# A GEGLU block with adaptive layer norm on Trainium2: a written plan for three engines in the gate and up passes, the differences on VectorE, and gb applied at the end of the down stage

## The chip, the core and the metric

The kernel runs on one core of one Trainium2 chip. The time is that of one execution on the device, in microseconds (us); the number given for a kernel is the median of its runs. The core has five engines that run their own instruction queues: TensorE (PE, with its weight loads as PEld), VectorE (DVE), ScalarE (ACT), GpSimd (POOL) and SyncE (SP), whose queue issues all the kernel's DMAs. An instruction that needs another engine's result waits for a semaphore at the head of its queue.

## The reference

T = 2048 tokens, D = 1024 columns, F = 3584 hidden columns, all in float32. It is cut here to what the change touches.

```python
mod = (silu(c) @ w_mod).reshape(1, 6, 1, -1)
sa, ca, ga, sb, cb, gb = (mod[:, i] for i in range(6))
h = layernorm(x) * (1 + ca) + sa
x = x + ga * attention(h)              # 32 heads, 4 segments with a running memory
h = layernorm(x) * (1 + cb) + sb
x = x + gb * ((gelu(h @ w_gate) * (h @ w_up)) @ w_down)
```

## The kernel before

**Stages.** Attention and its output projection come first, up to 1191.5 us in the profiled execution. The projection's last blocks (`projections`, `project`, L614 to L705) write x1, the sum after attention, to HBM; beside them the second norm writes h2, normalised and transposed, to HBM, and the first operands of the feed-forward part are cut. Then follow gate and up (L954, to 2363 us) and down (L1019, to the end).

**Numbers in two parts.** Each operand of a matmul is held as a high part (ScalarE copies float32 to the matmul's shorter type, L749) and a low part (the difference to the original, L751), and a product is three matmuls: high x high, high x low, low x high.

**Seven products instead of eight.** Gate and up of one block of 128 hidden columns are computed together as a 2 x 2 by 2 x 2 block product in a form with seven multiplications. The operands A are made from the blocks of h2 (two halves of D by two halves of 512 tokens); the operands B from the blocks of w_gate and w_up for these 128 columns (b11, b21 of gate, b12, b22 of up). Sums and differences of blocks stand in for the eighth product: for B four differences (`t1`, `t2_` and two more, L904 to L918), and as many for A. The products are numbered and run in the order `PRODUCTS = (1, 6, 2, 7, 5, 4, 3)`. The down stage does the same with sums of the hidden blocks and of w_down's blocks.

**Rounds.** There are two passes over the F columns, one for each half of the tokens (NP = 2, TP = 1024), with 28 blocks of 128 columns each (FC = 28): 56 rounds, numbered m = 0 to 55, in `gate_up(m)`. In a round each product is 12 matmuls of 128x128 by 128x512 (four pieces of 128 rows by three high and low pairings). Three PSUM banks `pa`, `pb`, `pc` take the products, and several products are added onto one bank: product 1 to `pa`, then ScalarE copies it to c1 (L979), then product 2 is added onto it. After product 6, 7, 5, 4 and 3 VectorE reads a bank (L981, L987, L989, L991, L994); TensorE may not add the next product onto a bank before it has been read. Such a reading is called a taking below. VectorE then multiplies the two GELU values by the two sums (L995, L996), and the result `g` is stored to HBM.

**Work beside the products.** Four kinds share the engines with the takings:

- `b_part(m + 2)`: the tables of a later round are loaded (`rg`, `ru`, 512 KB each), the four differences are made by GpSimd (`diff`, L762), the seven high parts by ScalarE, and the low parts by VectorE except two (products 5 and 3), which are GpSimd's.
- `w_parts`: in the first pass, for 14 pairs of w_down's blocks: VectorE multiplies them by gb (L938), GpSimd makes four differences (L762), and the results go to HBM as `wT_d`.
- the second norm for the second half of the tokens (`norm_tiles`, with TensorE's transposes `tpb`), the sums of its blocks (`a_mix`), and at the end of the first pass the 28 operands A for the second pass (`a_next`).
- `sum_part`: in the second pass, sums of a round's result with earlier ones (`sc`, L1014): two instructions in each of the first 14 rounds, six in each of the last 14.

**Order.** TensorE and SP run in the order in which the program is written. For SP the steps of `sides` (generators advanced by `step()` after every half product) and of `late` place the DMA issues. For VectorE, ScalarE and GpSimd a planner decides: it orders instructions by its own estimate of when they can start. Two further places matter. The operands A of the first pass are cut in `a_first`, `a_second` (before the stage, its rows in the two buffers `ra`, one pair at a time) and `a_last` (at its start). And the row gb, spread over all partitions by two pairs of matmuls with a matrix of ones (`row_parts`, L161), is computed at the start of the stage, between the first matmuls of round 0. In the down stage (`down`) the last additions read x1 and a PSUM bank and store the output: `final`, called first with no bank (GpSimd adds a stored sum to x1, L1083) and then with one (L1085).

Of the kernel before, what the change touches and what calls it, by code (L numbers as in the profile page):

```python
# [19 lines left out]
P = 128  # L20
D = 1024
# [15 lines left out]
def block_kernel(ctx: ExitStack, tc: tile.TileContext, x, c, wmod, wq, wkv, wo, beta, wg, wu, wd, out):  # L37
# [636 lines left out]
    def projections():  # L674
# [17 lines left out]
        sides.append([ff["b"](0), 2, "b"])  # L692
# [11 lines left out]
        next(ff["b1"])  # L704
# [14 lines left out]
    def feed_forward():  # L719
# [21 lines left out]
        A, B, hid, done = {}, {}, {}, set()  # L741
# [6 lines left out]
        def cut(hi, lo, src, eng, behind=False):  # L748
            i = [nc.scalar.activation(hi, src, AF.Copy)]  # L749
            for k in parts(src.shape[-1], eng):  # L750
                i.append(eng.tensor_sub(lo[:, k], src[:, k], f32(hi)[:, k]))  # L751
            if behind:
                keep(*i[:2])

# [5 lines left out]
        def diff(dst, a, b):  # L760
            for k in parts(dst.shape[-1], nc.gpsimd):
                nc.gpsimd.tensor_sub(dst[:, k], a[:, k], b[:, k])  # L762

        def put_a(p, i, kt, src, eng, behind=False):
            hl = [a_tile(i, kt, q, f"A{p}_{i}_{kt}_{q}") for q in range(2)]
            cut(hl[0], hl[1], src, eng, behind)
            A[p, i, kt] = hl
# [13 lines left out]
        def a_mix(p):  # L781

            for kt in range(4):
                r = rows(p, kt, ra_tile, "rm")
                for _ in range(4):
                    yield
                a11, a21, a12, a22 = r[0][:, :L], r[0][:, L:], r[1][:, :L], r[1][:, L:]
                s1 = tmp_tile(f"m1_{p}_{kt}")
                s2 = tmp_tile(f"m2_{p}_{kt}")
                for i, t, f in ((5, s1, lambda: nc.vector.tensor_add(s1, a21, a22)),  # L790
                                (6, s2, lambda: nc.vector.tensor_sub(s2, s1, a11)),
                                (7, a21, lambda: nc.vector.tensor_sub(a21, a11, a21)),
                                (3, a12, lambda: nc.vector.tensor_sub(a12, a12, s2))):
                    f()
                    later(3, lambda i=i, t=t, kt=kt: nc.sync.dma_start(mix_rows(i)[kt * P:(kt + 1) * P], t))
                    for _ in range(4):
                        yield

        def a_next(p):

            tok = p * TP
            todo = [(i, b) for i in PRODUCTS for b in range(2)]
            rs = []

            def load():
                q = len(rs)
                if q < len(todo):
                    i, b = todo[q]
                    src = (mix_rows(i) if i in MIX else
                           h2_d[0 if i == 1 else L:L if i == 1 else D, tok + (L if i == 4 else 0):tok + (TP if i == 4 else L)])  # L810
                    get = ra_tile if q % 3 == 2 else raw_tile
                    t = get(f"ra{p}_{i}_{b}").rearrange("p (k t) -> p k t", k=2)
                    nc.sync.dma_start(t, src[2 * b * P:(2 * b + 2) * P].rearrange("(k p) t -> p k t", p=P))
                    rs.append(t)

            for _ in range(5):
                load()
            yield
            for q, (i, b) in enumerate(todo):
                while (p * FC - 1, i) not in done:  # L820
                    yield
                for k in range(2):
                    put_a(p, i, 2 * b + k, rs[q][:, k], nc.vector)
                    if k:
                        load()
                    yield

        def a_first():
# [4 lines left out]
            for kt in range(4):  # L833
                r = rs[kt]
                a11, a21, a12, a22 = r[0][:, :L], r[0][:, L:], r[1][:, :L], r[1][:, L:]
                put_a(0, 1, kt, a11, nc.vector, True)
# [5 lines left out]
                put_a(0, 6, kt, s, nc.vector, True)  # L842
                yield
                put_a(0, 2, kt, a12, nc.vector, True)
# [6 lines left out]
        def a_second():  # L851

            rs = [rows(0, kt, ra_tile, "rb") for kt in range(1)]
            for _ in range(3):
                yield
            for kt in range(4):
                r = rs[kt]
                a11, a21, a22 = r[0][:, :L], r[0][:, L:], r[1][:, L:]
                s = tmp_tile(f"s5_{kt}")
                keep(nc.vector.tensor_add(s, a21, a22))  # L860
                nc.gpsimd.tensor_sub(a21, a11, a21)
                if kt < 2:
                    put_a(0, 4, kt, a22, nc.gpsimd)
                yield
                put_a(0, 7, kt, a21, nc.vector, True)
                yield
                put_a(0, 5, kt, s, nc.vector, True)
                if kt < 3:
                    rs.append(rows(0, kt + 1, ra_tile, "rb"))
                yield  # L870
                yield

        def a_last():

            r = ra_tile("rc").rearrange("p (k t) -> p k t", k=2)
            nc.sync.dma_start(r, h2_d[D - 2 * P:D, L:TP].rearrange("(k p) t -> p k t", p=P))
            for kt in range(4):
                (h2, l2), (h6, l6) = ([f32(t) for t in A[0, i, kt]] for i in (2, 6))
                s1 = tmp_tile(f"s1_{kt}")
                s2 = tmp_tile(f"s2_{kt}")  # L880
# [451 lines left out]
```

## Time and profile before

| what | value |
|---|---|
| median of 3 runs | 2915.62 us (2914.53 to 2917.37) |
| the profiled execution | 2912.03 us, its span 2910.3 us |
| granted TensorE clock in it | 0.985 of full speed |
| busy in the span: PE, DVE, ACT, POOL | 2771.3, 1671.9, 1310.4, 1179.4 us |
| gate and up | first matmul 1191.5 us, last one starts at 2362.6 us |
| DMA | 480.39 MB, 165 GB/s in the mean |

The profile is of one execution. In a table of windows each row gives a stretch of the span, its length, then the busy time of each engine with its number of instructions, the granted clock of TensorE, the mean busy share of the DMA queues' engines, and GB/s. A row of groups reads: line, engine, operation, output <- inputs, shape, count, then busy time and the mean time of one in ns, then the idle time of the engine just before them and what ended it. A row of waits reads: who waited <- for what: us in total, times, longest. A row of the timeline reads: start, length, engine, line, operation, and in brackets the idle time before it.

### The profile page before, as it was taken

To read this page: it belongs to the slowest core of one execution; us is meant where nothing else is said; L and a number is where in the kernel's file an instruction comes from. 1 tells how busy PE (TensorE), PEld (TensorE's weight loads), DVE (VectorE), ACT (ScalarE), POOL (GpSimd) and SP (SyncE) were. 2 spreads that over 40 slices of the span, in tenths; PEclk is the share of its full clock that TensorE was granted. 3 is DMA by queue.
4 is the path that set the end of the run, shared out by engine and by line. 5 is a ranking of instruction groups with operands and counts; after the bars stand their busy time and mean duration, and the time that the engine had idled before them with its cause. 6 is when DMAs were issued, how large, how long until landed. Compare 5 with 4: busy or idle time off the path is not lost.

```text
span 2910.3 us, 41951 instructions
## 1 busy us (share of the span) xinstructions
PE 2771.3 (95%) x14716; PEld 2286.9 (79%) x14716; DVE 1671.9 (57%) x3366; ACT 1310.4 (45%) x2871; POOL 1179.4 (41%) x1696
## 2 busy tenths in 40 slices
PE   5999999999999999799989998999999989999999
PEld 4788888888888787577767887888877778888887
DVE  7565666766666824555556555655677763334442
ACT  6677766676666634244422334333323233232221
POOL 0333334333343422466668763644566611102221
PEclk8999999999999999899999999999999999999999
DMA  7567666766555657455566434344456575544652
GB/s 239 113 131 145 144 109 131 145 137 115 108 112 98 168 174 232 147 196 202 188 210 222 164 113 167 144 145 145 171 227 239 223 244 185 195 145 147 202 187 92
DMA packets 229875, 480.39 MB, mean 165 GB/s; under 512 B 17696, under 2 KB 92448, under 8 KB 229664
## 3 DMA queue, kind: packets, MB, share of 16 engines
q1 hardware_dynamic: 229664, 477.72, 55.7%
q8 instruction: 115, 1.88, 0.3%
q14 instruction: 96, 0.79, 0.1%
HBM read 300.96 MB, written 126.35 MB: 147 GB/s over the span
## 4 chain that ended last, share of the span: by engine, by line
PE 69%; DVE 9%; POOL 7%; DMA 6%; ACT 4%; issue 4%; SPq 0%; DVEq 0%; POOLq 0%; ACTq 0%
PE f L962 25%; PE d L1142 18%; PE kv L365 10%; PE q L371 3%; PE y L626 3%; PE T L556 3%; POOL wt L762 3%; PE S L492 2%; PE O L565 2%; POOL t L762 2%; POOL B L751 1%; ACT sj L496 1%; DVE qs L509 1%; DMA wd<-wd 1%; DVE sj L494 1%
## 5 line engine op out<-in xcount | busy, mean ns | idle before, releaser
L962 PE MATMUL f<-A,B 128*128 128x512 f32 x4704 | 1098.0, 394 | 57.6 <-DVE c L981 34.6
L962 PEld LDWEIGHTS f<-A,B 128*128 128x128 f32 x4704 | 889.7, 190 | 258.8 <-DVE c L981 43.8
L1142 PE MATMUL d<-wb,ah 128*128 128x512 f32 x2352 | 536.6, 391 | 7.0 <-DVE wb L1052 3.7
L1142 PEld LDWEIGHTS d<-wb,ah 128*128 128x128 f32 x2352 | 443.5, 189 | 100.1 <-DVE wb L1052 4.2
L494 DVE CUSTOM_DVE_ANT_0 sj<-S,mask 128x384 f32<-128x384 f32 (+3 forms) x512 | 229.6, 487 | 226.1 <-PE S L492 207.6
L496 ACT ACTIVATE sj<-sj,mm 128x384 f32<-128x384 f32 (+3 forms) x512 | 281.4, 551 | 113.5 <-DVE mm L494 113.2
L559 POOL TENSOR_SCALAR_AFFINE_SELECT pt<-pt 128x128 f32<-128x128 f32 x512 | 170.7, 354 | 338.2 <-ACT pt L558 332.6
L749 ACT ACTIVATE B<-t 128x512 fp32r<-128x512 f32 x168 | 106.0, 631 | 291.8 <-PE f L962 219.7
L1052 DVE TENSOR_TENSOR ah<-ar,ah 128x1792 fp32r<-128x1792 f32 x56 | 118.5, 2116 | 196.6 <-ACT ah L1051 189.7
L1051 ACT ACTIVATE ah<-ar 128x1792 fp32r<-128x1792 f32 x56 | 95.3, 1702 | 278.5 <-PE d L1142 255.8
L365 PE MATMUL kv<-w,hha 128*128 128x256 f32 x1024 | 205.1, 286 | 3.4 <-ACT hha L334 3.4
L365 PE MATMUL kv<-w,hhh 128*128 128x256 f32 x1024 | 202.7, 286 | 0.0
L201 POOL TENSOR_TENSOR w<-r,w 128x256 fp32r<-128x256 f32 x180 | 133.3, 771 | 166.3 <-ACT w L196 166.2
L558 ACT ACTIVATE pt<-T 128x256 f32<-128x256 f32 (+3 forms) x512 | 181.9, 456 | 38.1 <-PE T L556 33.9
L365 PEld LDWEIGHTS kv<-w,hha 128*128 128x128 f32 x1024 | 167.7, 192 | 4.7 <-ACT hha L334 4.3
L365 PEld LDWEIGHTS kv<-w,hhh 128*128 128x128 f32 x1024 | 167.4, 193 | 0.3 <-issue 0.2
L751 POOL TENSOR_TENSOR B<-t,B 128x256 fp32r<-128x256 f32 x112 | 87.3, 800 | 167.3 <-ACT B L749 161.7
L365 PE MATMUL kv<-w,hla 128*128 128x256 f32 x512 | 146.4, 286 | 5.9 <-DVE hla L335 4.2
L556 PE MATMUL T<-qs,ks 128*128 128x256 f32 (+2 forms) x512 | 128.1, 360 | 20.1 <-DVE qs L509 7.6
L556 PEld LDWEIGHTS T<-qs,ks 128*128 128x128 f32 x512 | 80.8, 190 | 84.2 <-issue 35.1
L762 POOL TENSOR_TENSOR t<-rg,t 128x256 f32<-128x256 f32 x112 | 100.6, 918 | 111.1 <-DVE B L751 111.1
L365 PE MATMUL kv<-w,hlh 128*128 128x256 f32 x512 | 145.6, 284 | 0.0
(217 smaller groups left out, 4563.7 us busy)
## 6 DMA issues: line engine op xcount, KB each, us to landing
ar<-hid_d SPq DMA_DIRECT2D x56, 896.0 KB, 5.1
rg<-wg SPq DMA_DIRECT2D x56, 512.0 KB, 5.8
ru<-wu SPq DMA_DIRECT2D x56, 512.0 KB, 6.4
hid_d<-g SPq DMA_DIRECT2D x56, 512.0 KB, 2.7
sc<-hid_d SPq DMA_DIRECT2D x56, 512.0 KB, 5.0
hid_d<-sc SPq DMA_DIRECT2D x56, 512.0 KB, 3.1
br<-wT_d SPq DMA_DIRECT2D x49, 512.0 KB, 6.0
ks<-kh SPq DMA_DIRECT2D x64, 256.0 KB, 5.6
```

What stands on the lines that cost most here:

```text
L201: eng.tensor_sub(w[:, 1, k:k + 256], r[:, k:k + 256], f32(w[:, 0, k:k + 256]))
L365: nc.tensor.matmul(ps, b[:, sl], w[:, a], start=(kt == 0 and a == 0 and b is hi), stop=(kt == KT - 1 and a == 1), **kw)
L494: nc.vector.tensor_tensor_reduce(out=sj[:, :nv], in0=ps[:, :nv], in1=mask[:, L - nv:], scale=-1.0, scalar=3.4e38, op0=ALU.add, op1=ALU.min ...
L496: nc.scalar.activation(sj[:, :nv], sj[:, :nv], AF.Exp, bias=mm[:, j, i:i + 1], scale=-1.0, accum_out=ll[:, i, j:j + 1])
L556: nc.tensor.matmul(ps[:, :nn], ks[:, j, kc * P:(kc + 1) * P], qs[:, j, L - nn:], start=True, stop=True)
L558: nc.scalar.activation(pt, ps[:, nn - n:nn], AF.Exp)
L559: nc.gpsimd.affine_select(pt[:, :P], pt[:, :P], pattern=[[1, P]], compare_op=ALU.is_ge, fill=0.0, base=0, channel_multiplier=-1)
L751: i.append(eng.tensor_sub(lo[:, k], src[:, k], f32(hi)[:, k]))
L762: nc.gpsimd.tensor_sub(dst[:, k], a[:, k], b[:, k])
L962: nc.tensor.matmul(ps, B[m, i][:, a, kt * P:(kt + 1) * P], A[p, i, kt][b], start=(start and kt == 0 and a == 0 and b == 0), stop=(kt == 3 ...
L1052: nc.vector.tensor_sub(t[:, 1], r, f32(t[:, 0]))
L1142: nc.tensor.matmul(ps[t], ops[n][:, x, k, t * P:(t + 1) * P], b[:, y, kk % 2], start=(kk == 0 and x == 0 and y == 0), stop=(kk == 13 and x ...
```

## The change

- **A plan.** Within gate and up VectorE, ScalarE and GpSimd now run in the written order as TensorE and SP do, except in the last round and down, where the planner stays. Each piece of side work is a function entered at a place `(m, s)`: round m, step s of 14 (two steps to a product). After each half product `gate_up` calls what is entered there; where a product ends, its taking comes first.
- **GpSimd's differences and low parts** go to VectorE: the four differences and two low parts of B in each round, the four differences for each pair of w_down's blocks, those of A. GpSimd keeps four subtractions in round 0, seven low parts of A at the turn to the second pass, the powers of the norm, and its work in down.
- **gb** is no longer multiplied into w_down's blocks. The row is computed in the third part of the down stage, and `before` (GpSimd: product with gb, then addition to x1) and `final` (VectorE: product of the bank with gb, then addition) apply it.
- **Buffers and loads.** `a_second` alternates between the two `ra` buffers and two of the four `raw` buffers and loads two pairs of rows ahead. The tables of round 1 are loaded after the output projection rather than before its last block. The differences of B have three buffers of their own (`t`). The rows of A for the second pass go to `sc` and `ra` buffers. In down, x1 is loaded for two tiles at a time into `raw` buffers. The sums and stores of the last round are issued in the first part of down, behind the first cuts, instead of ahead of them.

The core of the diff (functions that only move to the plan with the same work, `norm_plan`, `mix_plan`, are left out):

```diff
-        sides.append([ff["b"](0), 2, "b"])
+        sides.append([ff["b"](), 2, "b"])
...
-        next(ff["b1"])
...
+        def at(m, s, *fs):
+            plan.setdefault(14 * m + s, []).extend(fs)
...
+        def less(eng, dst, a, b):
+            for k in parts(dst.shape[-1], eng):
+                eng.tensor_sub(dst[:, k], a[:, k], b[:, k])
+        def high(hl, src):
+            return nc.scalar.activation(hl[0], src, AF.Copy)
+        def low(hl, src, eng=nc.vector):
+            less(eng, hl[1], src, f32(hl[0]))
...
         def a_second():
-            rs = [rows(0, kt, ra_tile, "rb") for kt in range(1)]
+            rs = [rows(0, kt, (ra_tile, raw_tile)[kt % 2], "rb") for kt in range(2)]
...
-                nc.gpsimd.tensor_sub(a21, a11, a21)
+                nc.vector.tensor_sub(a21, a11, a21)
                 if kt < 2:
-                    put_a(0, 4, kt, a22, nc.gpsimd)
+                    put_a(0, 4, kt, a22, nc.vector)
...
         def a_last():
+            def one(kt):
...
+                at(0, 2 * kt, lambda: less(nc.gpsimd, s[1], l2, l6), lambda: less(nc.vector, s[0], h2, h6))
+                at(0, 2 * kt + 2, lambda: nc.vector.tensor_add(s[0], s[0], s[1]), lambda: high(hl, s[0]))
+                at(0, 2 * kt + 3, lambda: low(hl, s[0]))
+            def two(kt):
+                hl = new_a(0, 4, kt)
+                at(0, 2 * kt + 1, lambda: high(hl, r[:, kt - 2]))
+                at(0, 2 * kt + 2, lambda: low(hl, r[:, kt - 2]))
...
+        def b_plan(m, late=0):
+            q = m - 1
...
+            at(q, min(late - 8, -1 if m == 1 else 6), load)
+            at(q, late, lambda: sub(1, b12, b11))
+            at(q, late + 1, lambda: sub(2, b22, 1))
+            at(q, late + 4, lambda: sub(b12, b22, b12))
+            at(q, late + 6, lambda: sub(2, b21, 2))
+            for j, (i, n) in enumerate(zip(PRODUCTS, (b11, 2, b21, b12, 1, 2, b22))):
...
+                at(q, late + 2 * j + 1, hi)
+                at(q, late + 2 * j + 2, lo)
+        def w_plan(k):
+            m = 1 + 3 * k // 2
...
+            at(m, 0, load)
+            for q, s in enumerate((7, 9, 10, 11)):
+                at(m, s, lambda q=q: sums(q))
+            at(m, 13, store)
...
+        def a_plan():
+            tok, m = TP, FC - 1
...
+            for q in range(8):
+                at(m - 2, 6 + 2 * q, lambda q=q: load(q))
+            s = 2
+            for j, i in enumerate(PRODUCTS):
+                for kt in range(4):
+                    at(m, s, lambda i=i, kt=kt: hi(i, kt))
+                    at(m, s + 1, lambda i=i, kt=kt: lo(i, kt))
+                    if kt != 1 or j % 2:
+                        s += 1
...
         def gate_up(m):
...
+            taken = (lambda: nc.scalar.activation(c1, pa, AF.Copy),
+                     lambda: add(u2, pb, c1),
+                     lambda: nc.scalar.activation(g1, pa, gelu),
+                     lambda: add(u3, pb, c1),
+                     lambda: add(u3, pc, u3),
+                     lambda: (add(g2, pb, c1), nc.scalar.activation(g2, g2, gelu)),
+                     lambda: (add(u2, pc, u2), nc.vector.tensor_mul(g1, g1, u2)))
+            at(m, 12, lambda: nc.vector.tensor_mul(g2, g2, u3))
...
+            if p == 1:
+                at(m, 2, load)
+                for n, s in enumerate((1, 3) if fc < FH else (1, 3, 5, 7, 9, 10)):
+                    at(m + 1, s, lambda n=n: sums(n))
+                for n, s in enumerate((5,) if fc < FH else (5, 9, 12)):
+                    at(m + 1, s, lambda n=n: store(n))
+            at(m + 1, 3, lambda: nc.sync.dma_start(rows_of(i_, fc % FH), g))
...
                     if kt % 2 == 1:
-                        step()
+                        if kt == 3:
+                            taken[j]()
+                        for f in iter_plan(14 * m + 2 * j + kt // 2):
+                            f()
...
-        def down():
+        def down(rest):
...
+            def before(i, q):
...
+                    times(nc.gpsimd, y, o, gbb[:, cols_])
+                    for k in parts(L, nc.gpsimd):
+                        nc.gpsimd.tensor_add(x_[:, t, k], x_[:, t, k], y[:, k])
+            def final(i, t, ps, x_):
+                y = tmp_tile(f"yp{i}_{t}")
+                nc.vector.tensor_mul(y, ps, gbb[:, here[1]])
+                (nc.vector.tensor_sub if i == 4 else nc.vector.tensor_add)(x_, x_, y)
...
+                if n == 0:
+                    for f in rest:
+                        f()
+                if n == 2:
+                    row_of(gbb, modT[:, 40:48], tmp_tile, "gb")
...
         with tc.manual_schedule(engines={mybir.EngineType.SP}):
             next(ffn)
+            with tc.manual_schedule(engines={mybir.EngineType.DVE, mybir.EngineType.Activation, mybir.EngineType.Pool}):
+                next(ffn)
+            next(ffn)
```

Left of `w_parts`, whose multiplication goes:

```diff
-                for t in (a, b):
-                    nc.vector.tensor_mul(t, t, gbb)
...
-                    diff(dst, x_, y_)
+                less(nc.vector, *((c[:, :L], b12, b11), (c[:, L:], b22, b12), (d[:, :L], b22, c[:, :L]),
+                                  (d[:, L:], d[:, :L], b21))[q])
```

More of the change, by code (lines that the diff above doesn't have):

```diff
@@ L758, in keep, with new_a, put_a @@
                 tc.keep_in_program_order(i)
[L760 to L767, printed above, removed]
+        def less(eng, dst, a, b):
[5 more added lines that the diff above has]
+            less(eng, hl[1], src, f32(hl[0]))
+        def new_a(p, i, kt):
+            A[p, i, kt] = [a_tile(i, kt, q, f"A{p}_{i}_{kt}_{q}") for q in range(2)]
+            return A[p, i, kt]
+        def put_a(p, i, kt, src, eng):
+            hl = new_a(p, i, kt)
+            keep(high(hl, src))
+            low(hl, src, eng)
         def mix_rows(i):
@@ L779, in rows @@
             return r
[L781 to L826, printed above, removed]
         def a_first():
@@ L902, in b_part, with new_b, b_first, put @@
+        def new_b(m, i):
+            t = ffp[0].tile([P, 2, L], F32R, name=f"B{m}_{i}", tag="B", bufs=8)
+            B[m, i] = t
+            return t[:, 0], t[:, 1]
+        def b_first():
+            b11, b21, b12, b22 = b_views(0, raw_tile)
+            def put(i, src):
+                hl = new_b(0, i)
+                high(hl, src)
+                low(hl, src)
+            for _ in range(4):
                 yield
-            t1 = tmp_tile(f"t1_{m}")
-            diff(t1, b12, b11)
-            put(1, b11, nc.vector)
+            t1 = tmp_tile("t1_0")
+            t2_ = tmp_tile("t2_0")
+            less(nc.vector, t1, b12, b11)
+            put(1, b11)
@@ L957, in gate_up @@
             last = m == NP * FC - 1
-            def product(ps, i, start):
+            ps = {}
+            rows_of = lambda i, k: hid_d[i][k * P:(k + 1) * P]
+            get = raw_tile if last else sc_tile
+            pa, pb, pc = (s_ps(f"f{q}_{m}") for q in range(3))
+            c1, u2, u3 = (c_tile(f"c{q}_{m}") for q in range(3))
+            g = raw_tile(f"g{m}") if last else ffp[3].tile([P, TP], F32, name=f"g{m}", tag="g", bufs=2)
+            g1, g2 = g[:, :L], g[:, L:]
+            add = nc.vector.tensor_add
@@ L977, in gate_up @@
-            c1, u2, u3 = (c_tile(f"c{q}_{m}") for q in range(3))
-            product(pa, 1, True)
-            nc.scalar.activation(c1, pa, AF.Copy)
-            product(pb, 6, True)
-            nc.vector.tensor_add(u2, pb, c1)
-            product(pa, 2, False)
-            g = raw_tile(f"g{m}") if last else ffp[3].tile([P, TP], F32, name=f"g{m}", tag="g", bufs=2)
-            g1, g2 = g[:, :L], g[:, L:]
-            nc.scalar.activation(g1, pa, AF.Gelu_apprx_tanh)
-            product(pb, 7, False)
```

349 lines of the change are left out of this document (197 added, 152 removed).

## The prediction

> **What bounds the kernel now.** I read the page's totals first, then the windows of the gate and up stage, then the waits there, then prices.
>
> ```profile
> span 2910.3 us, 41951 instructions
> PE 2771.3 (95%) x14716; PEld 2286.9 (79%) x14716; DVE 1671.9 (57%) x3366; ACT 1310.4 (45%) x2871; POOL 1179.4 (41%) x1696
> ...
> L962 PE MATMUL f<-A,B x4704: 387/389/1415, 1191.5 to 2362.6; 128*128 128x512 f32 x196
> ```
>
> TensorE is busy for 95% of the span, so only its idle and its slow stretches can be won. The 4704 matmuls of gate and up start between 1191.5 and 2362.6 us; with 0.4 us for the last the stage takes 1171.5. Its windows, columns as in the first row:
>
> ```profile
> core 0: us, PE busy (x) PEld busy (x) DVE busy (x) ACT busy (x) POOL busy (x), PEclk, DMA share, GB/s
> 1191.50:1254.00 62.50, 45.43 (x164) 33.71 (x164) 40.12 (x49) 18.71 (x31) 42.70 (x43) 0.84 0.40 130
> 1254.00:1611.00 357.00, 330.08 (x1430) 267.36 (x1429) 213.48 (x269) 127.60 (x236) 241.77 (x281) 0.97 0.56 200
> 1611.00:1791.00 180.00, 178.90 (x789) 147.84 (x789) 91.07 (x117) 56.09 (x94) 105.47 (x126) 1.00 0.38 134
> 1791.00:1831.00 40.00, 30.60 (x121) 23.99 (x120) 33.64 (x45) 23.44 (x43) 19.94 (x23) 0.87 0.71 259
> 1831.00:2111.00 280.00, 280.00 (x1237) 231.89 (x1236) 160.71 (x213) 89.33 (x148) 146.40 (x179) 1.00 0.41 149
> 2111.00:2351.00 240.00, 226.93 (x988) 184.41 (x987) 174.65 (x211) 70.08 (x114) 141.74 (x136) 1.00 0.60 227
> ...
> L962 PE MATMUL f<-A,B 128*128 128x512 f32 x1237 | 280.6, 389 | 0.0
> ```
>
> From 1831 to 2111 TensorE never idles: 280.6 us by 1237 is the undisturbed pitch, 0.2268 us. A round (7 products of 12 matmuls) is then 84 x 0.2268 = 19.05 us and a step (half a product) 1.36. The six windows lose 17.1, 26.9, 1.1, 9.4, 0 and 13.1 us, 67.6 in all, and the granted clock drops to 0.84, 0.97 and 0.87 in some of them.
>
> ```profile
> PE f L962 <- DVE c L981: 34.6, 20, 6.4
> PE f L962 <- ACT c L979: 10.4, 4, 8.0
> PE gb L161 <- DVE gbdg L155: 10.0, 2, 9.8
> PE f L962 <- DVE c L989: 7.8, 4, 3.7
> PE f L962 <- DVE c L987: 4.5, 4, 2.9
> ```
>
> Total, times, longest: TensorE waits for VectorE or ScalarE to take a partial sum out of PSUM, and once for the gb row; these five are 67.3 of the 67.6 us. Why VectorE is late shows inside one late round:
>
> ```profile
> 2204.23 1.22 DVE L1014 TENSOR_TENSOR sc<-sc,g 128x512 f32<-128x512 f32 x1
> 2205.38 2.37 DVE L1014 TENSOR_TENSOR sc<-sc,sc 128x512 f32<-128x512 f32 x2
> 2207.67 0.68 DVE L751 TENSOR_TENSOR B<-t,B 128x512 fp32r<-128x512 f32 x1
> 2208.27 0.68 DVE L1014 TENSOR_TENSOR sc<-sc,sc 128x512 f32<-128x512 f32 x1
> 2208.87 0.68 DVE L981 TENSOR_TENSOR c<-f,c 128x512 f32<-128x512 f32 x1
> 2209.47 0.68 DVE L751 TENSOR_TENSOR B<-rg,B 128x512 fp32r<-128x512 f32 x1
> ...
> 2204.86 2.33 POOL L762 TENSOR_TENSOR ru<-ru 128x256 f32<-128x256 f32 x2
> ...
> L995 DVE TENSOR_TENSOR g<-g,c 128x512 f32<-128x512 f32 x55 | 55.9, 1016 | 0.1
> L981 DVE TENSOR_TENSOR c<-f,c 128x512 f32<-128x512 f32 x55 | 37.7, 686 | 26.6 <-PE f L962 26.6
> ```
>
> Five instructions that nobody waits for stand ahead of L981, and the three that run beside GpSimd's pair take some 1.2 us each; without GpSimd one takes 0.68 and starts 0.60 after the last. So two things delay the urgent instruction: its place, and GpSimd. L981, which reads PSUM, is hardly touched (0.686 in the mean of 55).
>
> **The change part by part.** *The floor.* 4704 x 0.2268 = 1066.9 us, and the norm's 64 transposes, which stay:
>
> ```profile
> L267 PE MATMUL tpb<-ident,nb 128*128 128x128 f32 x64 | 10.5, 290 | 0.0
> L161 PE MATMUL gb<-gbdg,ones 128*128 128x512 f32 x4 | 3.9, 1067 | 10.0 <-DVE gbdg L155 10.0
> ```
>
> Floor 1066.9 + 10.5 = 1077.4, which is 94.1 us under 1171.5: 67.6 of idleness, 3.9 of gb matmuls that leave for the down stage, and 22.6 left for the low clock. (1.00 less the clock, times its window, gives 62.5 x 0.16 + 357 x 0.03 + 40 x 0.13 = 25.9: it agrees.)
>
> *GpSimd's differences on VectorE.* Per round VectorE gets 4 differences and 2 low parts from GpSimd, beside the 7 sums and products and 5 low parts that it has: 18 instructions, and 4 more in the 14 rounds with a piece of w_down, 2 more in rounds 29 to 42 and 6 more from 43 on. GpSimd keeps nearly nothing in the stage, so the price is that of L981 or of the rows without GpSimd, 0.68 alone and 0.60 in a queue. The heaviest round is 24 x 0.60 to 24 x 0.68, 14.4 to 16.3 us, under 19.05. Cost to the path: none, with TensorE as cover.
>
> *The plan.* I laid it out by steps for a late round: at most two VectorE instructions per step (1.36 us at 0.68), and what takes a partial sum is first behind its product. Between takings stand 7, 3, 3, 2 and 7 others, 4.8, 2.0, 2.0, 1.4 and 4.8 us, where the matmuls give 5.4, 2.7, 2.7, 2.7 and 5.4. VectorE is idle when each product ends, and a bank isn't wanted again for a whole other product, 2.7 us. The 13.1 us of the last window and the 26.9 of the second go. ScalarE's high parts stand behind its own takings and are wanted 12 steps later; the tables' loads from HBM are issued 8 steps (10.9 us) ahead of their first use, against
>
> ```profile
> rg<-wg SPq DMA_DIRECT2D x56, 512.0 KB, 5.8
> ru<-wu SPq DMA_DIRECT2D x56, 512.0 KB, 6.4
> ```
>
> 5.8 and 6.4 us to land. SP stays in program order; each round's store of the sums, one step ahead of these loads, waits for a sum of step 3, so SP is past it at about step 4. Cost taken: 0, between 0 and 5.
>
> *The start.* By 1254.0 us 160 f and 4 gb matmuls were done in 62.5 us; 160 x 0.2268 + 3.9 = 40.2, so 22.3 are lost. The chain there goes through the one pair of buffers for the second A operands, four times; three of its loads:
>
> ```profile
> 1179.30 5.13 DMA rb<-h_d
> ...
> 1188.56 4.92 DMA rb<-h_d
> ...
> 1197.08 4.41 DMA rb<-h_d
> ...
> 1202.79 0.68 DVE L630 TENSOR_TENSOR xr<-y,xr 128x512 f32<-128x512 f32 x1
> 1202.92 2.08 PE L161 MATMUL gb<-gbdg,ones 128*128 128x512 f32 x2 [9.82 <-DVE gbdg L155]
> ```
>
> Now two pairs alternate, and the four loads need two turns of this chain, some 8.7 us each (1179.30 to 1188.56 less a little), instead of four: the last is issued about 15 us earlier, near 1182, and the last x row, queued on SP behind it, is no longer held by it. The gb row's 9.8 us go. What comes late instead: round 1's tables are no longer loaded ahead but on SP behind the last store of x1, which I put at about 1195, some 3 us after TensorE ends that tile (1191.5), and land 6.4 us later, about 1201.5; VectorE is to use them in step 4, which TensorE ends at 1191.5 + 5 x 1.36 = 1198.3. Behind that wait VectorE has six or seven instructions, about 4.4 us, then the taking that product 4 needs at 1205.2: late by 1.5, and the next, with round 0's 29 instructions, by 1.5 more. I take 5: 3 if the tables land in time, 12 if the last x1 store stays where the trace has it (1202.8).
>
> *The turn to the second half of the tokens* (9.4 us idle, 40 - 121 x 0.2268 = 12.6 lost with the clock): 21 of 28 low parts go between the others, 10 or 11 a round, so 28 or 29 x 0.60 to 0.68 is 17 to 19.7 us against 19.05. I take 2, of 0 to 13. *Rounds 20 to 23*, where SP must wait for a buffer to be stored before it loads the next: 1, of 0 to 3. *Clock* behind these: 1, of 0 to 3. Remainder 9, so the stage is 1077.4 + 9 = 1086.4, less by 85.1.
>
> On the clock, the last window has 12 pieces of 13.1 / 12 = 1.1 us at 1.00, the first has single ones up to 9.8 us at 0.84. The Trainium skill (TensorE: Matmul & The Clock Gate, Part 1) has the clock halved after an idle window of about 3.4 us, until as long a busy one; by that rule my small remainders would cost no clock and the sum would be lower by 1, which these rows support.
>
> *gb in the down stage.*
>
> ```profile
> 2371.00:2910.30 539.30, 535.56 (x2351) 442.98 (x2351) 207.85 (x151) 147.20 (x117) 86.02 (x80) 0.99 0.52 172
> ...
> L1085 DVE TENSOR_TENSOR xo<-xo,d 128x512 f32<-128x512 f32 x32 | 22.0, 688 | 84.9 <-PE d L1142 67.1 <-issue 17.9
> L1083 POOL TENSOR_TENSOR xo<-xo,w 128x256 f32<-128x256 f32 x32 | 40.8, 1307 | 96.4 <-DMA xo<-x_d 69.4 <-DVE u L1106 14.4 <-issue 12.5
> ```
>
> 32 products more on VectorE (22 us on 208 of 539) and 64 on GpSimd (64 x 1.31 = 84 on 86): per pair of tiles GpSimd needs 8 x 1.31 = 10.5 us and has 19, so both lie beside TensorE. The 28 multiplications by gb leave gate and up. The 4 gb matmuls cost their 3.9; 0.5 for a wait on their operand. The last tile has two instructions behind the last matmul: +0.6. The loads of x become half as many.
>
> *The boundary.*
>
> ```profile
> 2366.20 1.42 DVE L1014 TENSOR_TENSOR sc<-sc,sc 128x512 f32<-128x512 f32 x2
> 2367.54 2.02 DVE L1052 TENSOR_TENSOR ah<-ar,ah 128x1792 fp32r<-128x1792 f32 x1
> 2370.75 5.49 PE L1142 MATMUL d<-wb,ah 128*128 128x512 f32 x12 [3.66 <-DVE wb L1052]
> ```
>
> The last six sums now follow the first cuts instead of preceding them: -2, of -2.5 to 0. Before the stage, VectorE takes over a few differences: 0, of -3 to +3.
>
> *Sum.* -85.1 + 3.9 + 0.5 + 0.6 - 2 = -82.1, against this execution's own 2912.0 (span 2910.3): 2829.9. The three runs' median, 2915.6, is 3.6 above it, so 2833.
>
> **The rivals.** *The long places stay.* Start, turn and last window keep their 22.3, 12.6 and 13.1, because their operands or sums come late whatever the order: 48.0 instead of 9 gives 2872; half of it 2852. For it speaks that the first two are bursts of new operands; against, that all waits named are for takings.
>
> *VectorE becomes the bound* (slower than before). If its instructions kept the 1.02 us of L995, rounds of 24, 22 and 20 would exceed 19.05 by 5.4, 3.4 and 1.4, 14 of each: 143 us, so 2976. It decides from 0.96 us on, where 56 + 29 + 2 = 87 eat the gain. Against it: 0.68 in the rows without GpSimd. The Trainium skill (SBUF — State Buffer, Who interferes with whom) names a pair of SBUF ports that VectorE's two-input instructions and GpSimd hold in turns; by it 0.68 holds once GpSimd is silent, as the L1014 rows bear out.
>
> *A wait in front of each taking.* With the order fixed, a late table or high part stops all that is behind it on VectorE. 1.1 us, as in the last window, in each of 56 rounds gives 2833 + 61 = 2894; from 82 / 56 = 1.5 us on nothing is gained. For it: loads share the queue with stores at 0.60 of DMA's time; against it: 4.5 us of slack in the load's lead. The Trainium skill (TensorE: Matmul & The Clock Gate, Architectural detail) calls VectorE's queue strictly first in, first out, which is what such a wait needs; no row here shows one out of order.
>
> **How the numbers follow.** The forecast (2817 to 2850) 0.63; the long places stay (2850 to 2885) 0.20; a wait before each taking 0.09, half of it no gain; VectorE bound 0.05; under 2817, with nothing left and a better start, 0.03. The range 2817 to 2870 leaves out 0.2. About 0.2%, 6 us, is what a measurement can tell from no change: faster 0.90, same 0.02, slower 0.08.
>
> **What would show it.** Right: VectorE's low parts at about 0.69 in the mean, GpSimd near zero in the stage, the granted clock at 1.00 from the second round on, TensorE's waits for takings under 10 us. Wrong: VectorE waiting for a DMA or ScalarE just before a taking in many rounds, or its rows near 1 us.

## The result, and the profile after

| what | before | after |
|---|---|---|
| median of the runs | 2915.53 us (2914.53 to 2917.37) | 2827.94 us (2823.01 to 2830.36) |
| ratio | | 0.970 [0.968, 0.971] |
| the profiled execution, its span | 2912.03, 2910.3 us | 2830.36, 2828.7 us |
| granted TensorE clock | 0.985 | 0.995 |

The change makes the kernel 3.0% faster; 2833 us was forecast. Line numbers move. Of product 6 the taking is now L1084 (L981 before), of 7 L1086 (L987), of 5 L1087, of 4 L1088, of 3 and the first multiplication behind it L1089; low parts and differences are L759 (L751, L762), the late sums L1104 (L1014). First the totals of the page of after:

```profile
span 2828.7 us, 41301 instructions
PE 2747.5 (97%) x14716; PEld 2277.5 (81%) x14716; DVE 1779.7 (63%) x3761; ACT 1289.2 (46%) x2871; POOL 548.8 (19%) x986
...
PEclk9999999999999999999999999999999999999999
```

The matmuls of gate and up: shortest, median and longest in ns, then the first and the last start:

```profile
L1121 PE MATMUL f<-A,B x4704: 387/389/632, 1195.7 to 2277.9; 128*128 128x512 f32 x196
```

With 0.4 for the last matmul, gate and up take 1082.6 us instead of 1171.5: 88.9 less. The stage starts 4.2 later and the down stage is 3.1 longer: 88.9 - 4.2 - 3.1 = 81.6, the difference of the spans. Windows of after:

```profile
core 0: us, PE busy (x) PEld busy (x) DVE busy (x) ACT busy (x) POOL busy (x), PEclk, DMA share, GB/s
1195.70:1254.00 58.30, 57.10 (x250) 46.40 (x249) 46.77 (x76) 20.36 (x35) 4.64 (x5) 1.00 0.58 195
1254.00:1611.00 357.00, 357.00 (x1607) 295.50 (x1606) 257.52 (x421) 136.25 (x258) 6.22 (x7) 1.00 0.59 208
1611.00:1740.00 129.00, 129.00 (x571) 106.82 (x570) 92.75 (x143) 44.48 (x81) 6.43 (x6) 1.00 0.52 184
1740.00:1790.00 50.00, 46.30 (x193) 36.87 (x193) 40.82 (x61) 20.43 (x38) 8.14 (x8) 0.97 0.34 127
1790.00:2030.00 240.00, 240.00 (x1061) 198.72 (x1060) 159.91 (x250) 71.08 (x127) 0.00 (x0) 1.00 0.41 149
2030.00:2278.00 248.00, 248.00 (x1096) 205.24 (x1094) 192.20 (x305) 69.89 (x124) 0.00 (x0) 1.00 0.66 237
```

TensorE idles only in the first window (1.2 us) and at the turn (3.7). All its waits in the stage, 67.6 us before, are now these 4.9:

```profile
PE f L1121 <- DVE c L1086: 3.2, 2, 2.5
PE f L1121 <- DVE c L1084: 0.5, 1, 0.5
PE f L1121 <- DVE c L1087: 0.5, 1, 0.5
PE f L1121 <- ACT A L762: 0.4, 1, 0.4
PE f L1121 <- DVE A L759: 0.3, 1, 0.3
```

Groups of VectorE in gate and up, and behind them a stretch of its timeline in a late round:

```profile
L759 DVE TENSOR_TENSOR B<-t,B 128x512 fp32r<-128x512 f32 x165 | 113.9, 691 | 56.3 <-ACT B L762 56.3
L1084 DVE TENSOR_TENSOR c<-f,c 128x512 f32<-128x512 f32 x56 | 38.7, 691 | 40.8 <-PE f L1121 40.8
L1086 DVE TENSOR_TENSOR c<-f,c 128x512 f32<-128x512 f32 x56 | 38.7, 691 | 47.5 <-PE f L1121 47.5
```

```profile
2207.58 0.69 DVE L1084 TENSOR_TENSOR c<-f,c 128x512 f32<-128x512 f32 x1 [0.49 <-PE f L1121]
...
2209.99 0.68 DVE L1104 TENSOR_TENSOR sc<-sc,sc 128x512 f32<-128x512 f32 x1
2210.60 0.68 DVE L759 TENSOR_TENSOR t<-rg,t 128x512 f32<-128x512 f32 x1
2211.45 0.69 DVE L759 TENSOR_TENSOR B<-rg,B 128x512 fp32r<-128x512 f32 x1 [0.17 <-ACT B L762]
2213.02 0.69 DVE L1086 TENSOR_TENSOR c<-f,c 128x512 f32<-128x512 f32 x1 [0.88 <-PE f L1121]
```

At the taking of product 6 the roles are exchanged: VectorE has done its side work and waits for TensorE's product (0.49 us here, 40.8 in the 56 rounds), where L981 in before waited for TensorE only 0.5 us in all from 2085 to 2351 us. In front of the second taking it waits too (0.88 here, 47.5 in all), but it did so before (L987, 56.8 us). An instruction takes 0.69. The boundary to the down stage and the tail:

```profile
2281.43 1.42 DVE L1104 TENSOR_TENSOR sc<-sc,sc 128x512 f32<-128x512 f32 x2
2282.76 2.02 DVE L1170 TENSOR_TENSOR ah<-ar,ah 128x1792 fp32r<-128x1792 f32 x1
...
2822.95 0.69 DVE L1217 TENSOR_TENSOR yp<-d,gbb 128x512 f32<-128x512 f32 x1 [3.29 <-PE d L1280]
2823.74 0.69 DVE L1218 TENSOR_TENSOR xo<-xo,yp 128x512 f32<-128x512 f32 x1
```

The last sums (L1104) still run ahead of the first cut (L1170), and the last tile has one instruction more.

### The profile page after: what moved, and what is told of

It reads as the page before. It is cut to its first block, busy times and chain, and to the rows that moved or that the text cites. A ratio compares the mean times of both kernels' runs of the same rounds, so it can differ in the third digit from the quotient of the medians.

```text
span 2828.7 us, 41301 instructions
## 1 busy us (share of the span) xinstructions
PE 2747.5 (97%) x14716; PEld 2277.5 (81%) x14716; DVE 1779.7 (63%) x3761; ACT 1289.2 (46%) x2871; POOL 548.8 (19%) x986
## 4 chain that ended last, share of the span: by engine, by line
PE 81%; DVE 8%; ACT 4%; DMA 3%; issue 2%; POOL 1%; SPq 0%; DVEq 0%; POOLq 0%; ACTq 0%
PE f L1121 36%; PE d L1280 19%; PE kv L365 10%; PE y L626 3%; PE q L371 3%; PE T L556 3%; PE S L492 2%; PE O L565 2%; ACT sj L496 1%; DVE qs L509 1%; DMA x_d<-xr 1%; DVE sj L494 1%; ACT hta L272 1%; DMA r<-wkv 1%; PE R L581 1%
## 5 line engine op out<-in xcount | busy, mean ns | idle before, releaser
L1121 PE MATMUL f<-A,B 128*128 128x512 f32 x4704 | 1074.6, 390 | 4.9 <-DVE c L1086 3.2
L1170 DVE TENSOR_TENSOR ah<-ar,ah 128x1792 fp32r<-128x1792 f32 x56 | 115.9, 2070 | 183.6 <-ACT ah L1169 183.6
L1088 ACT ACTIVATE g<-g 128x512 f32<-128x512 f32 x56 | 35.4, 632 | 310.0 <-DVE g L1088 310.0
L759 DVE TENSOR_TENSOR B<-t,B 128x512 fp32r<-128x512 f32 x168 | 116.0, 690 | 56.4 <-ACT B L762 56.3
L1193 POOL TENSOR_TENSOR yo<-u,gbb 128x256 f32<-128x256 f32 x32 | 27.4, 882 | 560.5 <-ACT gbb L162 557.7
```

The lines of the kernel that those rows point to most:

```text
L759: eng.tensor_sub(dst[:, k], a[:, k], b[:, k])
L1121: nc.tensor.matmul(ps, B[m, i][:, a, kt * P:(kt + 1) * P], A[p, i, kt][b], start=(start and kt == 0 and a == 0 and b == 0), stop=(kt == 3 ...
L1170: nc.vector.tensor_sub(t[:, 1], r, f32(t[:, 0]))
```

## The experiments

My theory was the prediction's: the takings come late by their place on VectorE and by GpSimd beside it, so the order alone or the move alone recovers only a part. The rivals were that one of the two does it all, that removing the multiplications by gb matters by itself, and that VectorE has no room left. Each ratio is to runs of before in the same series (their medians are 2918.8 to 2920.6 us); 1% is 29.2 us. After itself ran beside 2915.5 us, so a distance to after by medians, given below, is uncertain by some 3 to 5 us. Where a run's idle is given by place, it is the length of a window less PE's busy time in it; the last window ends with the last matmul of the stage.

| kernel | median, us | ratio [95%] | idle: start, to 1611, to 2100, rest of stage |
|---|---|---|---|
| before | 2915.5 | 1 | 17.1, 26.9, 10.5, 13.1 |
| mul_kept | 2919.3 | 1.000 [0.999, 1.001] | 19.2, 27.3, 10.3, 13.9 |
| gb_only | 2891.3 | 0.990 [0.987, 0.993] | 16.5, 10.9, 9.6, 13.6 |
| old_places_move | 2851.2 | 0.977 [0.975, 0.979] | 12.3, 1.0, 10.4, 0 |
| neither | 2847.0 | 0.976 [0.974, 0.977] | 5.3, 6.8, 4.2, 0 |
| one_pair | 2836.6 | 0.972 [0.970, 0.974] | 6.9, 0, 3.7, 0.1 |
| order_only | 2829.9 | 0.969 [0.967, 0.971] | 3.3, 0, 4.5, 0 |
| move_only | 2825.6 | 0.968 [0.966, 0.970] | 3.5, 0.1, 2.6, 0 |
| after | 2827.9 | 0.970 [0.968, 0.971] | 1.2, 0, 3.7, 0 |

**order_only and move_only: one half of the change each.** In order_only B's four differences, two low parts and w_down's differences go back to GpSimd, and the written order stays; in move_only VectorE, ScalarE and GpSimd are left to the planner, and the differences stay on VectorE.

```diff
# order_only
-                less(nc.vector, pick(dst), pick(x_), pick(y_))
+                less(nc.gpsimd, pick(dst), pick(x_), pick(y_))
-                    low(v[i, "hl"], v[n] if n < 3 else v["b"][n - 3])
+                    low(v[i, "hl"], v[n] if n < 3 else v["b"][n - 3], nc.gpsimd if i in (5, 3) else nc.vector)
-                less(nc.vector, *((c[:, :L], b12, b11), (c[:, L:], b22, b12), (d[:, :L], b22, c[:, :L]),
+                less(nc.gpsimd, *((c[:, :L], b12, b11), (c[:, L:], b22, b12), (d[:, :L], b22, c[:, :L]),
# move_only
-            with tc.manual_schedule(engines={mybir.EngineType.DVE, mybir.EngineType.Activation, mybir.EngineType.Pool}):
-                next(ffn)
+            next(ffn)
```

> The changed kernel with the four differences and two low parts of B in each round, and the differences of w_down's blocks, given back to GpSimd; the plan stays. Theory (the place in the order is what made the takings late; GpSimd's slowing of VectorE alone costs little once a taking stands first): 0 to 25 us above the changed kernel, 2828 to 2853, TensorE's waits in gate and up under 20 us, although VectorE's instructions with two SBUF inputs return to 0.8 to 1.0 us in the mean. Rival (GpSimd's share of the work is the cause): 40 us or more come back, 2868 and above, waits of 40 us or more.

> The changed kernel without the written order on VectorE, ScalarE and GpSimd in gate and up: the planner orders them, the differences stay on VectorE. Theory (the place in the order): 20 to 60 us above the changed kernel, 2848 to 2890, with TensorE waiting 15 us or more for takings. Rival (GpSimd): VectorE at 0.69 us in the mean is quick enough in any order, under 10 us above, at most 2838.

Both are as fast as after; the intervals overlap. The price in order_only, by its groups of VectorE:

```profile
L1090 DVE TENSOR_TENSOR g<-g,c 128x512 f32<-128x512 f32 x56 | 67.1, 1198 | 0.7 <-ACT g L1088 0.7
L759 DVE TENSOR_TENSOR B<-t,B 128x512 fp32r<-128x512 f32 x110 | 105.4, 958 | 73.0 <-ACT B L762 72.6
```

The long durations (1198 and 958 ns) are back and cost next to nothing (the stage takes 1084.8 us, 2.2 more than in after), since the order puts a taking ahead of them. In move_only they are gone, and then the planner's order does as well as the written one. I had expected 20 to 60 us above after there: that was wrong.

**neither: both halves undone**, the two edits above together; left are the plan's places (handed to the planner), the buffers and loads, the differences of A on VectorE, and gb in the down stage.

> The changed kernel with both undone at once: the differences and two low parts of B and w_down's differences on GpSimd, and no written order on VectorE, ScalarE and GpSimd; the places of the plan stay as the order in which the planner is handed the work. Theory (a quick VectorE or a written order, one of the two is needed, and each alone removes the late takings): 25 to 65 us above the changed kernel, 2853 to 2893, TensorE waiting 20 us or more for takings. Rival (the places of the plan alone make the gain, whoever keeps the order): at most 10 above, at most 2838, waits under 12 us.

```profile
PE f L1121 <- DVE c L1084: 7.8, 5, 5.2
PE f L1121 <- ACT c L1083: 5.3, 4, 1.7
...
PE f L1121 <- DVE c L1086: 3.0, 1, 3.0
```

19 us above after by the medians, 17.1 by the length of the stage (1099.7 against 1082.6), less than the theory's lower end of 25. So some 70 of the 88 us come without either half, and either half brings the last 17 to 19. From 2100 us on no idle is left: there what stays of the change is enough, even with GpSimd at work. How the 70 divide between places, loads and buffers, beside what gb_only and one_pair show below, no run separates.

**gb_only and mul_kept: what the multiplications by gb cost.** gb_only is before with the one thing changed that gb is applied at the end of down. mul_kept is gb_only with the 28 multiplications kept, by a row of ones.

```diff
# gb_only, against before
-                    nc.vector.tensor_mul(t, t, gbb)
...
-        gb_row = row_parts(gbb, modT[:, 40:48], tmp_tile, "gb")
-        next(gb_row)
-        sides.append([gb_row, 1])
# mul_kept, against gb_only
+                    nc.vector.tensor_mul(t, t, one)
...
+        one = ffp[3].tile([P, D], F32, name="one")
+        nc.gpsimd.memset(one, 1.0)
```

> The kernel before with gb alone moved to the end of the down stage. Theory (two chains end near 1206 us at the start, the gb row's and that of the second A operands, so taking away one gains little): 0 to 9 us under the kernel before, 2907 to 2916; the 9.8 us wait at gb becomes a wait of 5 us or more for an operand A or a taking. Rival (the gb row is what delays the start): 10 us or more under it, at most 2905.

> The kernel before with gb moved to down as in gb_only, but the 28 multiplications of w_down's blocks on VectorE stay, by a row of ones. Theory (the multiplications, which wait for their load with takings behind them, are what gb cost in the first pass; the row at the start is not): most of gb_only's gain goes again, 2905 to 2918, TensorE's waits from 1254 to 1611 us back above 20 us. Rival (the row at the start): 2887 to 2897, as gb_only.

gb_only is 1.0% faster (29 us), where I had expected 0 to 9. mul_kept is at 1.000: the 28 multiplications carry all of it and the gb row at the start nothing, for there ScalarE's copy (L978, 8.9 us) takes the place of the wait for the row. The gain lies in the first pass; gb_only's window there has 107 matmuls more than that of before, 107 x 0.2268 = 24 us:

```profile
1254.00:1611.00 357.00, 346.12 (x1537) 283.21 (x1538) 199.48 (x266) 136.77 (x249) 248.82 (x303) 1.00 0.59 212
```

How the work behind the multiplications reaches TensorE shows in the timeline of before, ahead of its longest wait for a taking (6.41 us, to 1491.52):

```profile
1477.17 1.76 DVE L938 TENSOR_TENSOR wd<-wd,gbb 128x1024 f32<-128x1024 f32 x1
...
1489.64 1.22 DVE L751 TENSOR_TENSOR B<-t,B 128x512 fp32r<-128x512 f32 x1 [6.07 <-ACT B L749]
1490.79 0.68 DVE L981 TENSOR_TENSOR c<-f,c 128x512 f32<-128x512 f32 x1
...
1488.98 0.63 ACT L749 ACTIVATE B<-t 128x512 fp32r<-128x512 f32 x1 [8.61 <-POOL t L762]
...
1477.81 2.92 POOL L762 TENSOR_TENSOR wt<-wd 128x256 f32<-128x256 f32 x2
1480.69 2.33 POOL L762 TENSOR_TENSOR wt<-wd,wd 128x256 f32<-128x256 f32 x2
1482.98 1.88 POOL L762 TENSOR_TENSOR wt<-wd,wt 128x256 f32<-128x256 f32 x2
1484.82 1.40 POOL L762 TENSOR_TENSOR wt<-wt,wd 128x256 f32<-128x256 f32 x2
1486.19 1.40 POOL L762 TENSOR_TENSOR t<-ru,rg 128x256 f32<-128x256 f32 x2
1487.55 1.40 POOL L762 TENSOR_TENSOR t<-ru,t 128x256 f32<-128x256 f32 x2
```

Read it from below: GpSimd's four differences of w_down, which need the multiplications, stand ahead of its differences for B; ScalarE waits 8.61 us for one of those, VectorE 6.07 us for ScalarE's high part, and the taking L981 stands behind it. So here VectorE was not busy but waiting. At this place GpSimd itself began the differences without idle, behind a low part that lasted to 1477.85; over the stage its first differences of w_down wait 28.2 us for the multiplications (14 times), and the multiplications on VectorE wait 10.0 us for their own loads (9 times), with whatever stands behind them. In gb_only TensorE's wait in this round is still 4.10 us. What of the 29 us goes through GpSimd, what through those waits for loads and what through the multiplications' own 1.46 us each on VectorE, no run separates.

**old_places_move: gb_only, and the differences on VectorE in the old places** (old generators, planner and start).

```diff
-            for k in parts(dst.shape[-1], nc.gpsimd):
-                nc.gpsimd.tensor_sub(dst[:, k], a[:, k], b[:, k])
+            nc.vector.tensor_sub(dst, a, b)
-            put(5, t1, nc.gpsimd)
+            put(5, t1, nc.vector)
-            put(3, b22, nc.gpsimd)
+            put(3, b22, nc.vector)
```

> The kernel before with gb moved to down and all differences and low parts of gate and up's weights and of w_down on VectorE; the old generators, the planner and the old loads at the start stay. Theory (VectorE without GpSimd beside it is quick enough in any order): of the 2891 of gb alone 35 to 60 go, 2831 to 2856, what stays is the start's second A operands, 8 to 15 us of waits. Rival (the plan's places are needed as well): 2865 or more, waits of 30 us or more all through the stage.

40 us below gb_only: first pass and late rounds are clean (1.0 and 0), as the chain above lets expect once GpSimd is out of it. What is left is the start and the turn:

```profile
PE f L960 <- ACT c L977: 12.1, 2, 9.7
...
PE f L960 <- DVE c L979: 9.6, 2, 7.0
```

**one_pair: the second A rows with one pair of buffers again**, in after.

```diff
-            rs = [rows(0, kt, (ra_tile, raw_tile)[kt % 2], "rb") for kt in range(2)]
+            rs = [rows(0, kt, ra_tile, "rb") for kt in range(1)]
...
-                if kt < 2:
-                    rs.append(rows(0, kt + 2, (ra_tile, raw_tile)[kt % 2], "rb"))
+                if kt < 3:
+                    rs.append(rows(0, kt + 1, ra_tile, "rb"))
```

> The changed kernel with the rows for the second A operands in one pair of buffers again, loaded one ahead. Theory (four turns of load and cut return and end about 1206 us): 6 to 14 us above the changed kernel, 2834 to 2842, as waits for an operand A or a taking in round 0. Rival (the start was late for gb and for GpSimd alone): at most 2 above.

8.7 us above after by the medians, 7.4 by the length of the stage (1090.0), 5.7 of it as idle at the start. The intervals of the two ratios just overlap, so the size of what the buffers are worth beside the rest is rough; its place is clear.

**pool_load, pool_load2, dve_plus10: how much room VectorE has.** All three add work to after whose results nobody uses: pool_load twelve GpSimd subtractions in each of rounds 29 to 54, pool_load2 the same in rounds 30 to 54 but on an operand that the round itself makes, dve_plus10 ten more VectorE subtractions in each of rounds 43 to 54 (24 become 34).

```diff
# pool_load
+                        if 29 <= m < 55 and (2 * j + kt // 2) in (0, 2, 4, 6, 8, 10):
+                            a_, b_ = (f32(A[p, q_, 0][0]) for q_ in (1, 6))
+                            less(nc.gpsimd, tmp_tile(f"idle{m}_{j}"), a_, b_)
# pool_load2
+                        if 30 <= m < 55 and (2 * j + kt // 2) in (0, 2, 4, 6, 8, 10):
+                            idle = ra_tile(f"idle{m}_{j}")
+                            less(nc.gpsimd, idle[:, :L], f32(B[m, 3][:, 0]), f32(B[m, 3][:, 1]))
# dve_plus10
+                        if 43 <= m < 55 and (2 * j + kt // 2) in (0, 1, 2, 4, 5, 6, 8, 10, 11, 12):
+                            idle = ra_tile(f"idle{m}_{j}_{kt}")
+                            less(nc.vector, idle[:, :L], f32(B[m, 3][:, 0]), f32(B[m, 3][:, 1]))
```

> The changed kernel with 12 more GpSimd subtractions of 128x256 in each of rounds 29 to 54, as many as GpSimd had there before, of operands that are read only; their results are not used. Theory (VectorE beside GpSimd takes about 1.2 us for an instruction with two SBUF inputs, and 24 in a round then exceed 19.05 us by about 2): about 27 us above the changed kernel, 2838 to 2873, all of it in rounds 43 to 54, VectorE's mean there 0.85 to 1.0 us. Rival (the order alone makes the gain, VectorE has room for the slower instructions): 0 to 5 us above, at most 2833.

2996.5 us, 1.026 [1.024, 1.028], and it tells nothing of what it was made for. Nothing tied the subtractions to their rounds, so GpSimd ran them in one burst (to 1995 us), and VectorE's queue stood behind one instruction for down's gb row, which the planner had put far ahead and which needed a buffer of theirs:

```profile
1990.35 3.24 DVE L155 TENSOR_TENSOR gbdg<-ident,modT 128x512 f32<-128x512 f32 x1 [154.98 <-POOL idle L759]
```

> The changed kernel with 12 GpSimd subtractions of 128x256 added in each of rounds 30 to 54, six pairs at the steps 0 to 10, each reading an operand of its own round, so that they cannot run ahead; results unused. Theory (VectorE beside GpSimd takes about 1.15 us for an instruction with two SBUF inputs; 24 in a round then need about 21 of 19.05 us): 10 to 45 us above the changed kernel, 2838 to 2873, all of it in rounds 43 to 54. Rival (VectorE still has room): 0 to 5 above, at most 2833.

2849.7 us, 0.976 [0.974, 0.978], 21.8 above after, in the middle of the theory's 10 to 45. Its waits, and its groups of VectorE from 2030 to 2290 us:

```profile
PE f L1121 <- DVE c L1086: 16.7, 14, 2.5
```

```profile
L759 DVE TENSOR_TENSOR B<-rg,B 128x512 fp32r<-128x512 f32 x24 | 29.3, 1222 | 0.0
...
L1086 DVE TENSOR_TENSOR c<-f,c 128x512 f32<-128x512 f32 x12 | 8.1, 677 | 0.0
```

Up to round 42 the same GpSimd load costs nothing (1800 to 2030 us has no idle); with 24 instructions on VectorE a round takes 20.77 us, from one L1084 to the next (2038.68 to 2059.45), instead of 19.04, 20.8 in 12 rounds. In it VectorE waits only once, 1.22 us for ScalarE's high part, so it is the bound. Instructions with two SBUF inputs take 1.22 us beside GpSimd, takings, which read PSUM, 0.68. The Trainium skill (SBUF — State Buffer, Who interferes with whom) names a port pair that VectorE and GpSimd hold in turns as the only contention between engines; these rows agree, 1222 against 677 ns.

> The changed kernel with 10 more VectorE subtractions of 128x512 in each of the 12 rounds 43 to 54, 34 instead of 24, results unused. Theory (without GpSimd beside it VectorE takes 0.60 us for one in a queue): 34 x 0.60 = 20.4 against 19.05, so 1.35 x 12 = 16 us, 10 to 25 above the changed kernel, 2838 to 2853. Rival (each costs its whole 0.68 in the plan): 34 x 0.68 = 23.1, 49 us, 2870 to 2880.

2854.0 us, 0.977 [0.976, 0.979]: 26 above after by the medians, a little over the expected 25, and 19.5 by the spans. Its waits and its added work:

```profile
PE f L1121 <- DVE c L1084: 15.5, 12, 1.4
PE f L1121 <- DVE c L1086: 5.6, 13, 1.9
```

```profile
L759 DVE TENSOR_TENSOR idle<-B 128x512 f32<-128x512 f32 x120 | 82.2, 685 | 0.0
```

One round lies between two takings of product 6:

```profile
2075.65 0.68 DVE L1084 TENSOR_TENSOR c<-f,c 128x512 f32<-128x512 f32 x1
...
2096.94 0.68 DVE L1084 TENSOR_TENSOR c<-f,c 128x512 f32<-128x512 f32 x1
```

So a round takes 21.29 us instead of 19.04. Its 34 instructions start 0.60 apart, 20.4 us as the theory has it, and once VectorE waits 0.62 us for ScalarE, which the theory left out; the idle of TensorE that these waits show is only a part of the 2.25 us. At this rate 19.05 us hold some 30 instructions of VectorE (34 x 19.05 / 21.29); after's late rounds have 24.

**ar_first and ar_first_cuts: the boundary.** ar_first lays out down's buffers with that of the first load (`ar`) in front, which I took to come free earlier; ar_first_cuts also keeps the last six sums behind the first three cuts on VectorE.

```diff
# ar_first
-            SHAPES = {"w": (8, (L,), F32), ...
+            SHAPES = {"ar": (3, (7, 2 * P), F32), "w": (8, (L,), F32), ...
# ar_first_cuts, further
-                (nc.vector.tensor_add if plus else nc.vector.tensor_sub)(dst[:, h], a[:, h], b[:, h])
+                i = (nc.vector.tensor_add if plus else nc.vector.tensor_sub)(dst[:, h], a[:, h], b[:, h])
+                if last:
+                    keep(i)
...
+                if early:
+                    early.pop()
+                    keep(i)
```

> The changed kernel with the buffers of down laid out in another order, so that the first tiles of the hidden sums lie where product 1's operands were. Theory (at the boundary SP holds down's first load until product 4 of the last round gives the space free, and TensorE then idles 7 us): the load is issued 8 us or more earlier, the idle falls to 2 to 5 us, 2 to 6 us below the changed kernel. Rival (the tables of w_down, loaded behind it, or VectorE's sums set the boundary): 0 to 1 below.

> As ar_first, and the last six sums are kept behind the first three cuts on VectorE, which the changed kernel's text has but its planner undid. Theory (the sums hold back the first low part by some 2 us): 1 to 3 us below ar_first. Rival (the loads of w_down's tables set the boundary): no more than 1 below.

2832.0 and 2832.7 us, 0.970 for both: no gain. In ar_first the first load leaves at 2275.10, 2.4 us after the last matmul of gate and up starts (2272.7); in after it leaves at 2273.99, 3.9 us before it (2277.9). So this layout made the load later instead of earlier, TensorE waits 9.8 us for ScalarE's first cut, and the theory of an earlier load was not tested. In ar_first_cuts the order is as wanted, and the cut itself waits:

```profile
2284.63 2.02 DVE L1177 TENSOR_TENSOR ah<-ar,ah 128x1792 fp32r<-128x1792 f32 x1 [6.88 <-ACT ah L1176]
2286.58 2.35 DVE L1177 TENSOR_TENSOR wb<-br,wb 128x1024 fp32r<-128x1024 f32 x2
2288.85 1.29 DVE L1104 TENSOR_TENSOR sc<-sc,g 128x512 f32<-128x512 f32 x2
```

In this layout load and ScalarE's cut set the boundary, not the sums. In after's own layout ScalarE's first cut ends at 2280.63 and VectorE's low part starts at 2282.76, directly behind the sums, so there the order may cost 2.1 us; no run undoes it there. None of the twelve kernels is clearly faster than after.

## Why the prediction was right, and where its steps were not

*The floor* held to the digit: 1077.4 us were predicted, and PE's busy times in the six windows above add up to 1077.4. The last digit is luck, since that busy time also holds matmuls at a low clock (below). VectorE's low parts stand at 0.69, GpSimd is busy for 25 us of the stage (4.64 + 6.22 + 6.43 + 8.14), the clock is at 1.00 outside the turn, and the waits for takings are 4.2 us: all as named but for the turn. VectorE had room (some 30 instructions to a round), so the rival by which it becomes the bound stayed away; pool_load2 shows its mechanism, 20.8 us a round, but only with GpSimd kept at work. A wait in front of each taking did not come: in front of the first four VectorE waits for TensorE. Nor did the long places stay; old_places_move, whose start and turn keep 22.7 of before's 27.6 us (17.1 + 10.5), shows that they do when only the differences move.

*The remainder*, 9 us forecast, was 5.2 (1082.6 - 1077.4). The start was sized too large: 1.2 instead of 5. The tables of round 1 were issued at 1194.1 and 1195.5, near the predicted 1195, but not for the predicted reason: the last two stores of x1 stand behind them on SP (1196.7 and 1201.4), not ahead. They landed in some 4 us instead of 6.4, TensorE was itself 4 us later, and only 0.72 and 0.47 were lost at the takings. The turn was sized too small: 3.7 of idle instead of 2, 2.5 of it in one wait for L1086. VectorE is busy there for 20.8 of 21.5 and 20.2 of 23.1 us. These two rounds (L1084 at 1725.1 to L1084 at 1769.7) together take 44.6 us where two undisturbed ones take 38.1, so the turn costs 6.5 in all; the part that isn't idle lies in PE's busy time. Rounds 20 to 23 cost nothing that shows. The clock does cost something: the window of the turn has 0.97, and in it the stretches from 1756 to 1758 and from 1758 to 1760 us have 0.64 and 0.51, though the longest wait, just before them, is 2.52 us; by the Trainium skill's rule (TensorE: Matmul & The Clock Gate, Part 1: half speed after an idle window of about 3.4 us) it would have stayed at 1.00. These rows differ, and no run says why.

*Ahead of the stage* 0 was predicted (-3 to +3), and +4.2 came. It looks like scatter rather than the change: the stage starts at 1191.5, 1195.1, 1192.5 and 1192.8 us in before, gb_only, mul_kept and old_places_move, and in after and the nine kernels made from it anywhere from 1191.8 (ar_first) to 1197.4 (pool_load2).

*The down stage* came out at +3.1 for +3.0, by terms that were off. **The boundary failed:** -2 was predicted since the sums are written behind the first cuts. But there the planner orders VectorE, and it put them in front again; TensorE's idle is 7.5 us for 7.0 before. The gb matmuls cost 1.9 instead of 3.9, without a wait, and the tail more: from the last matmul's end to the end of the span 5.8 us instead of 3.7, 0.8 for the second instruction and 1.3 for a longer last store.

**The step that was wrong in its reasons** is the sentence that "the 28 multiplications by gb leave gate and up", to which the sum gives no price. Taken out alone they bring 29 of the 88 us. The sum came out since it was made from the floor upwards, in which every idle microsecond goes, whatever removes it; the reasons for each share were not tested by it. I had read the late rounds, where VectorE is busy with five instructions in front of L981, and taken the first pass to be alike. There the row in front of L981 has 6.07 us of waiting for ScalarE, at the end of a chain through GpSimd's differences of the multiplied blocks. And order and move were treated as two parts that add up; the runs show either one to be enough (order_only and move_only), on top of places, loads and multiplications that bring 70.

## What to carry to other kernels

A floor (count times undisturbed pitch) with a small remainder predicts the time well when every loss is of one kind, but it doesn't say which edit removes it: price each edit by itself, and follow a late instruction back to the end of its chain in each stage, not in one. What an in-order queue delays is the urgent instruction behind a waiting one; either taking the slow producer out of that chain or ordering the urgent instruction in front removes it, and the second of the two then brings nothing more. A written order only holds where the planner is off: at the boundary the text was changed, the instructions were not.

## What the runs showed of the hardware

Idle TensorE is granted half its clock: in pool_load's long wait a window shows 0.50,

```profile
1900.00:1980.00 80.00, 0.00 (x0) 0.00 (x0) 0.00 (x0) 0.00 (x0) 80.00 (x118) 0.50 0.00 0
```

and the float32 matmuls of the gb row (L161) took 1067 ns in the mean at before's start, where the window's clock is 0.84, but 592 ns in after's down stage. VectorE's instructions of 128x512 last 0.68 us each yet follow one another at 0.60; in dve_plus10 nearly whole rounds of 34 run so, with one wait of 0.62 in them. And one instruction that the planner moved ahead (the gb row's, at 1656.8 us in after, 650 us before it is needed) cost nothing there and 155 us in pool_load, where its buffer was not yet free.
